# One batch more turned by DMA, named places and a new order in a fused attention and channel-mix kernel

## The chip, the cores and the metric

The kernel runs on one core of a Trainium2 chip. The metric is the device time of one launch in microseconds. The core has a matrix engine (TensorE, PE in the profile, whose weight loads stand apart as PEld), a vector engine (VectorE, DVE), an engine for functions of one element (ScalarE, ACT), GpSimd (POOL) and SyncE (SP). Each has its own instruction stream and works it off in order; they wait for each other through semaphores. Sixteen DMA engines move data. Here POOL issues all loads from HBM, and SP the stores and the transposing transfers.

## The reference

Eight batches, 8 heads, 576 tokens, 64 numbers in each head. First a linear attention with a normalization, then a channel mix over the 512 columns of all heads:

```
kv  = einsum('bhsd,bhse->bhde', k, v)
out = einsum('bhsd,bhde->bhse', q, kv)
x   = out / sqrt(mean(out * out, axis=-1) + 1e-06) * g_norm     # heads side by side: 8 x 576 x 512
x_prev = x shifted by one token, zeros first
xk = mu_k * x + (1 - mu_k) * x_prev
xr = mu_r * x + (1 - mu_r) * x_prev
k2 = max(xk @ w_k, 0)                                           # 512 x 1024
v2 = k2 * k2 @ w_v                                              # 1024 x 512
result = 1 / (1 + exp(-(xr @ w_r))) * v2                        # w_r: 512 x 512
```

Inputs and output are fp32 in HBM; the kernel computes its products in bf16.

## The kernel before

Batches are counted from one in this text and from 0 in the code, so "batch four" is `a == 3`. A batch's 576 tokens are held as 9 groups of 64. Two batches share the buffers of the channel mix: a pair of batches has 9 output tiles of 128 rows, and `V.1.4` in the order means output tile 4 of the pair that batch `1` belongs to.

The work of a batch goes through these steps. The words are those of the order, the functions those of the code.

- `ld.n.b`: one load by POOL, k, v or q (n = 0, 1, 2) of batch b, cast to bf16 on the way (L194). Odd-numbered batches in the code (`b % 2`) lie in three tiles of their own, `in_k`, `in_v` and `in_q`, one each; the even ones reuse `sq0` for k, `qT0` for v and `q0` for q. A load waits until the batch two before it has done with the place.
- `kv`: 72 products of 64x64 on TensorE that make k'v (L287), and `kvo`, two evacuations from PSUM to SBUF.
- q turned, so that its columns lie on the partitions. Batches two to four: `qt`, 72 transposes on TensorE into PSUM (L330), and `qto`, four evacuations. From batch five on (`a >= QD`, with `QD = 4`): `qd`, one transposing DMA from SBUF to SBUF issued by SP (L302), in which pairs of heads come to lie otherwise, so that `kvs` adds a copy of k'v with its upper and lower 64 partitions exchanged (two copies of 64x256, L297). Batch one has code of its own.
- `u`: the products of q and k'v. Without the transposing DMA these are 40 products (L352), with it 72 smaller ones (L316, `u_turned`).
- `sq`, `red`, `nw`, `mul`: squares on ScalarE, their sums, a root by Newton steps and the multiply on VectorE.
- `x`, `xo`, `x0`, `x0o`: the result turned back on TensorE and moved to `xT`; for the last three batches `yd` does this by a transposing DMA (L409) and `gx` multiplies by g.
- `wrap`, `dif`, `sc`, `add`: the token shift and the two mixes xk and xr.
- `K` (`Ka`, `Kz`, `Kp` for the first two batches): products with w_k (L631, L708), each with a relu evacuation on ScalarE or VectorE; `ks` (`ksp`) squares them.
- `R`: product with w_r (L653) and its sigmoid on ScalarE into a tile `sig`.
- `V` (`Vq`): half or quarter of an output tile's product with w_v (L663); `fin` multiplies it by `sig` on VectorE (L676) and has SP store its two halves (L684).
- `L`: the very last output tile, in two column parts of 256 (L671), stored by SP and ACT.
- `wm`: TensorE products that compute nothing, at the start.

The order of all this is written out by hand in `ORDER`, a list of stages made of such words; each word issues its instructions in turn, so this list is the order on every engine and queue. A quote mark behind a word gives the operation to VectorE instead of ScalarE. The digits behind `=` name the PSUM banks that it takes, out of eight. A wait stands where data or a place demand it.

Tiles of the pool `work` rotate: a name has a number of buffers (two as a rule, 7 for `rt`, 6 for `sig`, 7 for `out`), and a new tile takes the one used longest ago.

The places that matter for the change are at the end of the second stage of `ORDER`. The old order has `kv.3`, then `qt.3.1 ... qt.3.0` and their evacuations, `x.2.0.4`, half tiles of `V.1`, and `u.3.1` and `u.3.0` at the beginning of the third stage.

Of the kernel before, what the change touches and what calls it, by code (L numbers as in the profile page):

```python
# [9 lines left out]
FP32 = mybir.dt.float32  # L10
# [9 lines left out]
    cast.0' cast.1' kvc.0.2=01 kvco.1' kvco.0 qtc.0.2=23 qtco.1' cols=4 qtco.0 wm.1.0=1 uc.1=5 sqc.1 uc.0=6  # L20
    qtc.2.2=70 qtco.3' msc.1=1 sqc.0 msc.0=3 qtco.2' rsc.1 wm.1.1=0 kvc.2.1=4 kvco.2 wm.1.2=1 uc.4=2 rsc.0 mcc.1
    uc.2=0 wm.1.3=5 kvc.3.1=7 mcc.0 sqc.2 kvco.3' sqc.4 difh.0.0.256.576 sc.0.0.1.256.576' msc.2=1 uc.3=4
    sc.0.0.0.256.576' uc.5=5 sqc.3 msc.4=3 wm.1.4=7 msc.3=6 rsc.2 add.0.0.0.256.576 wm.1.5=7 Ka.0.4=7 Ka.0.5=1
    rsc.3 mcc.2 mcc.3 dih.0.2.256.576 dih.0.3.256.576 sqc.5 rsc.4 Ka.0.3=6 msc.5=0 fu.0.0.2.256.576 Ka.0.2=4
    fu.0.0.3.256.576 Ka.0.0=3 rsc.5 Ka.0.1=0 Kz.0.4 mcc.4 mcc.5 Kz.0.1 wrap.0 Ka.0.6=2 difh.0.1.0.256 Kz.0.2
    difh.0.0.0.256 sc.0.1.2 Kz.0.0 Kz.0.5' fu.0.0.3.0.256 Ka.0.7=7 fu.0.0.1.0.256 fu.0.0.2.0.256 Kz.0.6 sc.0.1.1
    qt.1.0=50 Kz.0.3' fu.0.0.0.0.256 qto.1.0.1 Kz.0.7 ksp.0.0.0.4' qto.1.0.0' kvh.0=41 kvho.0.0 Kp.0.1.1'=3
    kvho.0.1 Kp.0.1.0'=2 uh.1.0=60 ksp.0.0.4.8 sqh.1.0.0 uh.0.0=74 ld.1.2 uh.2.0=1 sqh.0.1.0 ksp.0.1.0.4'
    sqh.0.0.0 sqh.1.1.0 ld.0.2 sqh.2.0.0 redh.5.9.0 Kp.0.1.2=5 redh.0.5.0 rsh.5.9.0 mulh.0.0.0 Kp.0.1.3=3
    rsh.0.5.0 Vq.0.1.0=2 mulh.0.1.0 ld.2.2 Vq.0.1.1 ksp.0.1.4.8 sc.0.1.3' mulh.2.0.0 Vq.0.2.0=5 qt.1.1=37  # L30
    xh.2.2.0=41 mulh.1.1.0 Vq.0.2.1 xho.2.2.0.0 qto.1.1.1' mulh.1.0.0 qto.1.1.0' xho.2.2.0.1 kvh.1=07 kvho.1.1'
    x0h.0=46 kvho.1.0 x0ho.0.1 x0ho.0.0' xh.0.2.0=13 uh.0.1=07 xho.0.2.0.1' uh.1.1=46 xho.0.2.0.0' sqh.0.0.1
    sqh.0.1.1 uh.2.1=3
    """,
    """
    Vq.0.1.2 add.0.1.1 sqh.2.0.1 sqh.1.0.1 sqh.1.1.1 redh.5.9.1 rsh.5.9.1 Vq.0.2.2 redh.0.5.1 mulh.0.1.1
    Vq.0.3.0=1 rsh.0.5.1 Vq.0.3.1 ld.2.3 mulh.0.0.1 mulh.2.0.1 sc.0.1.0 Vq.0.2.3 Vq.0.3.2 xh.2.2.1=70 add.0.1.0
    mulh.1.0.1 Vq.0.0.0=3 xho.2.2.1.1 mulh.1.1.1 Vq.0.0.1 xho.2.2.1.0 dif.1.384.576 sc.1.0.2.384.576'
    sc.1.0.1.384.576' Vq.0.0.2 sc.1.0.3.384.576 Vq.0.0.3 sc.1.0.0.384.576' adda.1.0.384.576 xh.0.2.1=07
    xho.0.2.1.1' x0h.1=46 x0ho.1.1' xho.0.2.1.0 wrap.1 x0ho.1.0 dif.1.0.384 sc.1.0.3.0.384' Vq.0.3.3  # L40
    sc.1.0.0.0.384' ld.1.3 Vq.0.1.3 tab sc.1.1.3' R.0.1=0 fin.0.1 Kp.1.0.3=4 Kp.1.0.2=7 sc.1.0.2.0.384'
    add.1.0.1.0.384 Kp.1.0.0'=6 sc.1.1.1 Kp.1.0.1'=0 R.0.0=4 sc.1.0.1.0.384' add.1.0.0.0.384 ld.0.3 R.0.2=7
# [12 lines left out]
    K.2.2.1=2 u.3.1=10 fin.1.5 u.3.0=47 u.3.2=3 sq.3.1.1 sq.3.0.0 fin.1.7 add.2.1.0 sq.3.2.0 fin.1.4 sq.3.1.0
    K.2.0.1'=5 K.2.1.1=2 K.2.3.1=6 sq.3.0.1 add.2.1.1 red.3.0.5 red.3.5.9 nw.3.0.1 nw.3.1.2 nw.3.2.3 K.2.6.0=5
    nw.3.3.4 R.2.1=2 ld.2.6 R.2.3=6 nw.3.4.5 K.2.1.0=5 K.2.3.0=2 V.1.8.0=6 nw.3.5.6 nw.3.6.7 K.2.6.1=5 V.1.8.1
    ks.2.1 nw.3.7.8 mul.3.1.0 K.2.5.0=2 mul.3.1.1 mul.3.0.1 mul.3.0.0 mul.3.2.0 K.2.2.0=5 K.2.0.0=1 kv.4=02
    ks.2.0' kvo.4.0 fin.1.8 x.3.0.4=75 x0.3=41 K.2.7.0=3 K.2.5.1=0 kvo.4.1 ks.2.2 ks.2.3' x0o.3.1' xo.3.0.4.1'
    kvs.4.1' R.2.2=6 wrap.3 K.2.4.1=1 xo.3.0.4.0' x0o.3.0' dif.3 sc.3.0.3' sc.3.0.2' sc.3.1.2' K.2.4.0=3 ld.0.6  # L60
    ks.2.4 ks.2.5' R.2.0=5 sc.3.0.1 ks.2.6 sc.3.0.0' V.2.2.0=0 ld.1.6 K.2.7.1=2 add.3.0.1 sc.3.1.0' kvs.4.0
    V.2.0.0=7 V.2.1.0=6 u.4.0=41 u.4.1=35 ks.2.7 qd.5 add.3.0.0 V.2.1.1 sc.3.1.3
    """,
    """
    K.3.4.0'=2 sq.4.1.1 ld.2.7 V.2.0.1 sq.4.0.0 sq.4.0.1 fin.2.0 V.2.2.1 K.3.2.1=2 fin.2.1 fin.2.2 red.4.5.9
    K.3.7.0'=7 sq.4.1.0 K.3.6.0=6 sc.3.1.1 add.3.1.1 K.3.7.1=2 ks.3.7' K.3.2.0=0 K.3.5.0=6 K.3.3.0=7 add.3.1.0
    K.3.4.1=2 u.4.2=0 sq.4.2.0 red.4.0.5 nw.4.0.1 nw.4.1.2 kv.5=67 nw.4.2.3 nw.4.3.4 kvo.5.0 ld.0.7 kvo.5.1
    K.3.0.0=2 nw.4.4.5 K.3.5.1=6 ks.3.4 ld.1.7 nw.4.5.6 kvs.5.0' nw.4.6.7 nw.4.7.8 R.3.6=7 K.3.1.0=2 K.3.0.1=6
    K.3.1.1=7 kvs.5.1' ks.3.5 mul.4.1.0 ks.3.2 mul.4.0.0 K.3.6.1=2 K.3.3.1=6 mul.4.2.0 mul.4.1.1 R.3.7=7
    V.2.3.0=3 mul.4.0.1 ks.3.6' ks.3.0 V.2.3.1 ks.3.3' ks.3.1 x0.4=40 fin.2.3 x0o.4.0 x.4.0.4=25 u.5.2=6  # L70
    u.5.1=71 x0o.4.1' xo.4.0.4.1' u.5.0=43 xo.4.0.4.0 V.3.6.0=0 sq.5.0.1 sq.5.0.0 sq.5.2.0 wrap.4 sq.5.1.0 dif.4
    sc.4.0.3 V.3.6.1 fin.3.6 red.5.5.9 sq.5.1.1 red.5.0.5 V.3.5.0=5 R.3.5=2 nw.5.0.1 nw.5.1.2 sc.4.0.0 qd.6
    sc.4.0.1' nw.5.2.3 V.3.5.1 nw.5.3.4 sc.4.1.3 sc.4.0.2 R.3.4=0 add.4.0.0 V.3.8.0=2 V.3.8.1 nw.5.4.5 R.3.8=0
    fin.3.5 nw.5.5.6 nw.5.6.7 sc.4.1.0 V.3.4.0=5 add.4.0.1 V.3.4.1 nw.5.7.8
    """,
    """
    K.4.7.0=0 mul.5.1.0 mul.5.1.1 K.4.1.1=7 K.4.5.1=1 K.4.4.0=0 mul.5.0.1 mul.5.0.0 mul.5.2.0 sc.4.1.1 add.4.1.0
    K.4.6.0=3 kv.6=74 sc.4.1.2' K.4.4.1=1 ks.4.4 K.4.0.1'=6 K.4.2.0'=0 add.4.1.1 kvo.6.1 K.4.5.0'=3 K.4.2.1'=1
# [40 lines left out]
def kernel(  # L119
# [16 lines left out]
    C = H * HD  # L136
# [689 lines left out]
```

## Time and profile before

| | us |
|---|---|
| median of 3 runs | 199.12 (198.38 to 199.41) |
| the profiled execution, in all | 198.45 |
| its span, from first to last instruction | 196.7 |

The page gives, for each engine, its busy time and its share of the span. TensorE has 2387 products in 185.8 us, VectorE 356 instructions in 163.0 us. The line of the DMA cuts the span into 40 slices of 4.9 us, with the busy share of the sixteen transfer engines in tenths. The chain of waits is followed from the last instruction back to what released it. In a timeline the first number is the start in us from the beginning of the span and the second the duration; a transfer's entry is its issue, not its landing. Groups of instructions are named by line, output and inputs. Some that the change touches, with mean durations of one instruction in this execution:

| group | mean us |
|---|---|
| evacuation of turned q, 128x576: ScalarE / VectorE | 0.645 / 0.450 |
| swapped copy of k'v, 64x256: ScalarE / VectorE | 0.403 / 0.304 |
| last multiply of the output, 128x512 / 128x256 | 0.684 / 0.424 |
| relu evacuation, 128x320, VectorE | 0.490 |
| transposing DMA of y, from issue to landing, with no loads in flight | 4.9 to 6.6 |

### The profile page before, as it was taken

How to read it: one execution, taken by the hardware profiler on the slowest of the kernel's cores; microseconds unless marked ns; L12 is line 12 of the kernel's file. 1: busy time of each engine (PE TensorE's matmuls, PEld its weight loads, DVE VectorE, ACT ScalarE, POOL GpSimd, SP SyncE). 2: the span in 40 equal slices, each digit the busy share in tenths (PEclk: the TensorE clock that was granted, in tenths of full speed). 3: DMA queues.
4: the chain of work that ended last, by engine and by line, in shares of the span. 5: the costliest groups of instructions: out<-in, count | busy, mean ns of one | idle time of the engine just before them, and what ended most of it. 6: DMA issues, size and time to landing. Idle time of an engine off the chain costs nothing.

```text
span 196.7 us, 5776 instructions
## 1 busy us (share of the span) xinstructions
PE 185.8 (94%) x2387; PEld 111.1 (56%) x2409; DVE 163.0 (83%) x356; ACT 134.1 (68%) x275; POOL 27.6 (14%) x44
## 2 busy tenths in 40 slices
PE   7788899999999999999999999999999999999991
PEld 2435565665564667567554775676445666764450
DVE  2488899996999999978999899899899997876241
ACT  2375898779969867969987658989855557532310
POOL 7953343004021004002100000000000000000000
PEclk9999999999999999999999999999999999999999
DMA  5999999999999998999999378335723842005654
GB/s 212 219 211 206 202 205 208 207 217 243 230 230 208 220 189 223 224 170 268 154 215 202 81 136 171 86 80 29 176 45 58 182 107 57 0 0 130 140 144 124
DMA packets 38030, 31.51 MB, mean 160 GB/s; under 512 B 18924, under 2 KB 32500, under 8 KB 38004
## 3 DMA queue, kind: packets, MB, share of 16 engines
q0 software_dynamic: 14400, 16.19, 49.3%
q1 hardware_dynamic: 23204, 14.43, 33.5%
q10 hardware_dynamic: 400, 0.52, 0.8%
q8 instruction: 19, 0.31, 0.6%
q14 instruction: 7, 0.06, 0.1%
HBM read 33.56 MB, written 9.44 MB: 219 GB/s over the span
## 4 chain that ended last, share of the span: by engine, by line
PE 80%; DVE 9%; DMA 4%; issue 2%; ACT 2%; SPq 0%; DVEq 0%; POOLq 0%
PE ps_v L663 28%; PE ps_km L631 28%; PE ps_r L653 15%; DMA q<-in_q_dram 3%; PE ps_kv L287 2%; PE ps_u L316 1%; DVE y L420 1%; PE ps_x L435 1%; DMA out_dram<-out_sb 1%; DVE xT L512 1%; DVE out_sb L676 1%; PE ps_u L352 1%; DVE ss L361 1%; DVE sqk L639 1%; PE ps_qt L330 1%
## 5 line engine op out<-in xcount | busy, mean ns | idle before, releaser
L663 PE MATMUL ps_v<-wv_sb,sqk 128*128 128x512 bf16 x266 | 64.8, 379 | 1.0 <-issue 0.3
L631 PE MATMUL ps_km<-xk,wk_sb 128*128 128x288 bf16 (+3 forms) x480 | 64.0, 285 | 0.0
L631 PEld LDWEIGHTS <-wk_sb 128*128 128x128 bf16 x480 | 45.7, 98 | 16.2
L663 PEld LDWEIGHTS <-sqk 128*128 128x128 bf16 x280 | 26.7, 98 | 29.5 <-issue 0.6
L623 ACT ACTIVATE rt<-ps_km 128x288 bf16<-128x288 f32 (+3 forms) x81 | 33.5, 427 | 12.6 <-PE ps_km L631 9.0
L653 PE MATMUL ps_r<-wr_sb,xr 128*128 128x512 bf16 x136 | 34.9, 379 | 0.5
L656 ACT ACTIVATE sig<-ps_r 128x512 bf16<-128x512 f32 x36 | 21.2, 596 | 18.9 <-PE ps_r L653 18.6
L676 DVE TENSOR_TENSOR out_sb<-ps_v,sig 128x512 f32<-128x512 f32 (+1 forms) x37 | 24.3, 670 | 9.3 <-PE ps_v L663 7.7
L637 ACT ACTIVATE sqk<-rt 128x576 bf16<-128x576 bf16 (+4 forms) x32 | 23.4, 746 | 4.4 <-DVE rt L625 4.2
L601 ACT ACTIVATE m<-dx,cols 128x576 bf16<-128x576 bf16 (+1 forms) x30 | 21.7, 756 | 4.2 <-DVE dx L595 4.0
L625 DVE TENSOR_SCALAR rt<-ps_km 128x288 bf16<-128x288 f32 (+3 forms) x39 | 17.8, 473 | 6.6 <-PE ps_km L631 5.0
L653 PEld LDWEIGHTS <-xr 128*128 128x128 bf16 x144 | 13.9, 98 | 14.2
L361 DVE TENSOR_REDUCE ss<-sq 128x16 f32<-128x1024 bf16 (+1 forms) x12 | 15.8, 1344 | 0.4 <-ACT sq L357 0.4
L357 ACT ACTIVATE sq<-ps_u 128x512 bf16<-128x512 f32 (+1 forms) x30 | 14.6, 556 | 0.0
L618 DVE TENSOR_TENSOR xr<-m,xT 128x1152 bf16<-128x1152 bf16 x16 | 11.9, 750 | 0.8 <-ACT m L601 0.8
L639 DVE TENSOR_TENSOR sqk<-rt 128x576 bf16<-128x576 bf16 (+3 forms) x25 | 11.7, 482 | 0.7 <-ACT rt L623 0.6
L595 DVE TENSOR_TENSOR dx<-xT 128x2304 bf16<-128x2304 bf16 (+5 forms) x13 | 11.4, 893 | 0.4
L603 DVE TENSOR_SCALAR m<-dx,cols 128x576 bf16<-128x576 bf16 (+3 forms) x36 | 11.4, 346 | 0.2
L618 DVE TENSOR_TENSOR xk<-m,xT 128x1152 bf16<-128x1152 bf16 (+2 forms) x16 | 10.9, 699 | 0.2
L420 DVE TENSOR_TENSOR y<-ps_u,rs 128x512 bf16<-128x512 f32 (+1 forms) x15 | 8.4, 628 | 0.1
L217 ACT CAST kv<-ps_kv 128x128 bf16<-128x128 f32 (+1 forms) x15 | 3.3, 244 | 6.9 <-PE ps_kv L472 5.7
L261 PE MATMUL ps_warm<-zeros 128*128 128x512 bf16 x18 | 6.9, 502 | 1.2 <-DVE eps L224 1.2
(91 smaller groups left out, 162.2 us busy)
## 6 DMA issues: line engine op xcount, KB each, us to landing
out_dram<-out_sb SPq DMA_DIRECT2D x67, 128.0 KB, 3.2
qT<-in_v_dram POOLq DMA_DIRECT2D x3, 576.0 KB, 14.4
sq<-in_k_dram POOLq DMA_DIRECT2D x3, 576.0 KB, 12.9
q<-in_q_dram POOLq DMA_DIRECT2D x3, 576.0 KB, 10.8
in_q<-in_q_dram POOLq DMA_DIRECT2D x3, 576.0 KB, 7.9
in_v<-in_v_dram POOLq DMA_DIRECT2D x3, 576.0 KB, 14.3
in_k<-in_k_dram POOLq DMA_DIRECT2D x3, 576.0 KB, 11.8
wk_sb<-in_moe_w_k_dram POOLq DMA_DIRECT2D x2, 512.0 KB, 9.1
```

The costliest lines, as they stand in the source:

```text
L357: ACT.activation(out=sq[:, rg(t0, n, i) if n else slice(0, 1)], in_=held["u", a, part, i][1], func=AF.Square)
L361: DVE.tensor_reduce(out=ss[:, g0:g1], in_=sq[:, g0:g1], op=ALU.add, axis=AX.X)
L601: eng.activation(out=out_, in_=in_, func=AF.Copy, scale=mu)
L618: DVE.tensor_add(out=dst, in0=m[:, hs, c0:c1], in1=x[:, hs, c0:c1])
L623: eng.activation(out=dst, in_=ps, func=AF.Relu)
L625: eng.tensor_scalar(out=dst, in0=ps, scalar1=0.0, scalar2=None, op0=ALU.max)
L631: nc.tensor.matmul(ps[:, n, :], wk_sb[:, cc, 128 * fc:128 * fc + 128], at[b]["xk"][:, cc, c0:c1], start=(cc == 0), stop=(cc == NHP - 1))
L637: eng.activation(out=sqk[:, fcs, o:o + n], in_=src, func=AF.Square)
L653: nc.tensor.matmul(ps, xr[:, cc, 128 * t:128 * t + 128], wr_sb[:, cc, :], start=(cc == 0), stop=(cc == NHP - 1))
L656: ACT.activation(out=sig[b, t], in_=give("r"), func=AF.Sigmoid)
L663: nc.tensor.matmul(ps, sqk[:, fc, 128 * t:128 * t + 128], wv_sb[:, fc, :], start=(fc == 0), stop=(fc == NFC - 1))
L676: DVE.tensor_mul(out=o, in0=give(key), in1=sig[b, t][:, c])
```

## The change

Three things in the functions, and the whole of `ORDER` is written anew.

1. `QD` goes from 4 to 3: batch four's q is turned by the transposing DMA instead of TensorE, its u uses the 72 small products, and its k'v gets the swapped copy.
2. Work tiles get names with a number in them, one buffer to each name: by the parity of the batch for the tiles of a batch, by a list of free numbers for `rt` (7), `sig` (6) and `out` (7), from which a tile takes the number that was given back first.
3. The last output tile is cut into columns 0 to 383 and 384 to 511 instead of two halves. The order takes the smaller one first (`L.1 ... L.0`).

```diff
     def mine(a, key, shape, dtype, tag=None):
         if key not in at[a]:
-            at[a][key] = work.tile(shape, dtype, tag=tag or key, name=tag or key)
+            name = f"{tag or key}{key[1] if tag else a % 2}_"
+            at[a][key] = work.tile(shape, dtype, tag=name, name=name, bufs=1)
         return at[a][key]
...
-    QD = 4
+    QD = 3
...
+    free = {"rt": list(range(7)), "sig": list(range(6)), "out": list(range(7))}
+    place = {}
+
+    def slot(kind, key, shape, dtype):
+
+        n = place[kind, key] = free[kind].pop(0)
+        return work.tile(shape, dtype, tag=f"{kind}{n}_", name=f"{kind}{n}_", bufs=1)
+
+    def leave(kind, key):
+        free[kind].append(place.pop((kind, key)))
...
-            rts[b, fc] = work.tile([128, S], BF16, tag="rt", name="rt", bufs=7)
+            rts[b, fc] = slot("rt", (b, fc), [128, S], BF16)
...
-        c = slice(C // 2 * part, C // 2 * part + C // 2)
+        c = (slice(0, 3 * C // 4), slice(3 * C // 4, C))[part]
```

From the order, what lies around batch four. Before, the end of the second stage and the beginning of the third:

```
... R.1.5=1 mul.2.0.0 R.1.4=7 mul.2.1.0 mul.2.1.1 V.1.4.0=6 x0.2=10 x0o.2.1 kv.3=37 x0o.2.0 ld.1.4 qt.3.1=40
qto.3.1.0' qt.3.0=21 kvo.3.0 ld.2.5 x.2.0.4=35 ksp.1.1.6.8' xo.2.0.4.1' ld.0.5 xo.2.0.4.0 qto.3.0.0
V.1.6.0=4 qto.3.0.1 V.1.6.1 wrap.2 qto.3.1.1 V.1.7.0=5 dif.2 sc.2.1.2' sc.2.0.1 sc.2.0.0 sc.2.1.0 ld.1.5
fin.1.6 sc.2.1.3 sc.2.0.2' sc.2.0.3' V.1.5.0=3 add.2.0.0 kvo.3.1 V.1.4.1 add.2.0.1 V.1.5.1 qd.4 V.1.7.1
sc.2.1.1
--
K.2.2.1=2 u.3.1=10 fin.1.5 u.3.0=47 u.3.2=3 sq.3.1.1 ...
```

After, from the last tile of the first pair to u of batch four and on:

```
... Kp.1.1.4'=1 fin.0.3 u.2.0=63 sq.2.0.0 sq.2.0.1 Kp.1.1.5=0 qd.3 ld.2.4 red.2.5.9 ...
...
nw.2.6.7 nw.2.7.8 ksp.1.1.4.6 V.1.4.0=5 mul.2.0.1 mul.2.1.1 V.1.6.0=0 kv.3=37 mul.2.2.0 mul.2.1.0 x0.2=14
ksp.1.1.6.8 ld.0.5 mul.2.0.0 x.2.0.4=26 kvo.3.1' x0o.2.1' x0o.2.0 xo.2.0.4.0 kvo.3.0' xo.2.0.4.1' wrap.2
kvs.3.1 dif.2 kvs.3.0 V.1.5.0=7 sc.2.0.0 ld.1.5 sc.2.0.1 V.1.4.1 fin.1.4 sc.2.1.2' sc.2.0.2' u.3.0=41
u.3.1=36 sq.3.1.1 sc.2.0.3' sq.3.0.1 sc.2.1.1 V.1.7.0=2 sq.3.1.0 add.2.0.1 V.1.6.1 add.2.0.0 V.1.7.1 V.1.5.1
qd.4 fin.1.7 sc.2.1.3 fin.1.5
```

On SP's queue the transposing DMA of batch four stands behind the eight stores of the first pair's tiles 0 to 3, and that of batch five two stores behind it. The loads of batches three and four stand in the order k, v, q, then k, q, v; before they stood v, k, q, then q, v, k. At the start, the last fused multiply-adds that make xk of batch one's lower columns (`fu.0.0.n.0.256`) stand ahead of the last three `Kz` and their relu evacuations (one on VectorE); before, the last of the four stood behind seven of the eight `Kz`, two of those seven evacuated by VectorE. The number of warm-up products in `wm` goes from 6 to 9. From batch five on the steps are those of before, in another order.

More of the change, by code (lines that the diff above doesn't have):

```diff
@@ L38 @@
[L38 to L42, printed above, removed]
@@ new lines @@
+    add.6.1.0
+    """,
+    """
+    K.6.1.0'=7 K.6.1.1'=1 add.6.1.1 yd.7 K.6.3.0'=6 K.6.2.1=2 K.6.7.0=7 gx.7.0' fin.5.7 K.6.4.0=1 K.6.6.0=2
+    ks.6.1 gx.7.1' K.6.3.1=6 K.6.4.1'=7 K.6.0.1=1 R.6.3=2 K.6.2.0=6 R.6.2=5 wrap.7 V.5.8.0=1 ks.6.2 dif.7
+    K.6.0.0=7 K.6.6.1'=2 sc.7.0.2 sc.7.0.0' sc.7.0.1' add.7.0.0 sc.7.0.3 sc.7.1.3 V.5.8.1 ks.6.3 K.6.5.0=6
+    fin.5.8 add.7.0.1 K.6.5.1=5 R.6.0=7 R.5.5=2 ks.6.0'
+    """,
+    """
+    K.7.5.1'=1 fin.5.5 K.7.6.0=6 K.7.6.1=5 V.6.3.0=7 K.6.7.1'=2 ks.6.7 K.7.7.0'=1 ks.6.6' R.6.1=6 ks.6.4
@@ L109 @@
+    sta.7.7 L.1=2 L.0=0
     """,
@@ L654, in r @@
                              start=(cc == 0), stop=(cc == NHP - 1))
-        sig[b, t] = work.tile([128, C], BF16, tag="sig", name="sig", bufs=6)
+        sig[b, t] = slot("sig", (b, t), [128, C], BF16)
         ACT.activation(out=sig[b, t], in_=give("r"), func=AF.Sigmoid)
@@ L674, in finish @@
     def finish(b, t, key, c=slice(0, C), queues=(nc.sync, nc.sync)):
-        o = outs[b, t] = work.tile([128, c.stop - c.start], FP32, tag="out", name="out_sb", bufs=7)
+        o = outs[b, t, c.start] = slot("out", (b, t, c.start), [128, c.stop - c.start], FP32)
         DVE.tensor_mul(out=o, in0=give(key), in1=sig[b, t][:, c])
@@ L678, in finish @@
             store(b, t, i, q_, c)
+        if c.stop - c.start == C:
+            leave("sig", (b, t))
     outs = {}
@@ L683, in store @@
         bb, j = b - b % 2 + (2 * t + i) // G, (2 * t + i) % G
-        q_.dma_start(out=out[bb].rearrange("(p j) c -> j p c", j=G)[j, :, c], in_=outs[b, t][half(i), :])
+        q_.dma_start(out=out[bb].rearrange("(p j) c -> j p c", j=G)[j, :, c], in_=outs[b, t, c.start][half(i), :])
+        if i == 1:
+            leave("out", (b, t, c.start))
     PARTS0 = ((4 * P, S), (0, 4 * P))
```

136 lines of the change are left out of this document (65 added, 71 removed).

## The prediction

> **What bounds the kernel now.** I read three views in this order: the busy times with the chain of waits, then the timelines of the two engines that issue transfers, then the pieces of the chain around batch four.
>
> The page first. TensorE is busy 94% of the span, and the chain that ended last is 80% TensorE work:
>
> ```profile
> PE 185.8 (94%) x2387; PEld 111.1 (56%) x2409; DVE 163.0 (83%) x356; ACT 134.1 (68%) x275; POOL 27.6 (14%) x44
> ...
> DMA  5999999999999998999999378335723842005654
> ...
> PE 80%; DVE 9%; DMA 4%; issue 2%; ACT 2%; SPq 0%; DVEq 0%; POOLq 0%
> ```
>
> So TensorE work removed anywhere after the start is worth its own time, and a wait of TensorE costs its own length, because its stream is in order. The digits of the DMA say the second thing: until slice 22 (about 108 us) the transfer engines have no free time.
>
> Next, who issues transfers (start, length of the issue, queue, what):
>
> ```profile
> 28.63 0.74 POOL L194 DMA_DIRECT2D in_q<-in_q_dram  x1 [1.56 <-PE ps_x L435]
> ...
> 46.28 0.74 POOL L194 DMA_DIRECT2D q<-in_q_dram  x1 [14.98 <-PE ps_qt L330]
> ...
> 57.69 0.74 POOL L194 DMA_DIRECT2D in_q<-in_q_dram  x1 [9.18 <-PE ps_qt L330]
> ...
> 59.15 0.77 POOL L194 DMA_DIRECT2D in_v<-in_v_dram  x1
> 75.39 0.74 POOL L194 DMA_DIRECT2D q<-in_q_dram  x1 [15.48 <-DMA qT<-q]
> ...
> 76.86 0.77 POOL L194 DMA_DIRECT2D qT<-in_v_dram  x1
> 92.04 0.74 POOL L194 DMA_DIRECT2D in_q<-in_q_dram  x1 [14.41 <-DMA qT<-in_q]
> ```
> ```profile
> 63.01 7.81 SPq L302 DMA_TRANSPOSE qT<-q  x1
> ...
> 77.10 9.88 SPq L302 DMA_TRANSPOSE qT<-in_q  x1
> ```
>
> This gives the price of what the change adds. The transpose of batch five is issued at 63.01, and the load that waits for it goes at 75.39: 12.4 us. That of batch six: 77.10 to 92.04, 14.9 us. Both had loads beside them, v of batch six (issued 59.15, landing 14.3 later) until 73.4, and v of batch seven (76.86, 13.4 later) until 90.2. Each transpose is over 2.0 and 1.8 us after the last of these loads: here it ends when the loads let it.
>
> Last, the chain around batch four (start, length):
>
> ```profile
> 54.97 0.86 PE ps_v L663 x4
> ...
> 56.00 0.71 PE ps_kv L287 x72
> 56.71 0.65 PE ps_qt L330 x72
> 57.36 0.57 PE ps_x L435 x32
> ...
> 64.38 0.49 PE ps_km L631 x4
> 64.87 0.81 PE ps_u L352 x40
> ...
> 82.36 0.67 PE ps_u L316 x64
> ```
>
> k'v at 56.00, the transposes of q on TensorE, and u (q times k'v) only at 64.87.
>
> **The change part by part.** The sum is made against the profiled execution: 198.45 us, a span of 196.7 and 1.75 around it. The median of the three runs is 199.12, 0.67 above it.
>
> (a) The 72 TensorE transposes of q of batch four go: 0.65 us by the chain. With them go four evacuations (0.645 on ScalarE, 0.45 on VectorE each); two swapping copies of k'v (0.403 and 0.304) come. These lie off the chain, beside TensorE work, so I count nothing; uncovered, they would be a gain of 0.5 to 2.0. The 40 products of u become 72 small ones: 0.81 before, 0.67 for 64 of those 72 in the later batches, so 0.75 for all. Together -0.7.
>
> (b) Start. Batch one's lower k columns start at 22.31 on TensorE behind VectorE's last fused multiply-add, 21.70 to 22.17. Two relu evacuations of 0.49 stood in front of it; the new order puts one behind and gives one to ScalarE. VectorE was also idle for 0.94 before the first of them. I take 0.8 of this 0.98 + 0.94; bounds 0 and 1.9. The three added warm-up products (0.2 to 0.4 each) fill TensorE's wait for w_k, which lands at 15.0 in both: 0, and 1.2 if that cover is gone. So -0.8.
>
> (c) The new wait. When does u of batch four come up in the new order? Up to it the old TensorE list has these in addition: the transposes (0.65), four half tiles of the v product (4 x 0.86), one k product (0.49). 64.87 - 0.65 - 3.44 - 0.49 = 60.3; less (b), 59.5. When is its q there? The new list loads k, q, v for batch four where the old one had q, v, k, all issued by 31 and served in turn, so q takes the place of v: 29.82 + 19.9 = 49.7. SP's queue also has to pass the two stores of the tile before, which I put at 49 to 50 (in the old order such stores went at 48.5 to 50.9). So the transpose goes at about 50.0. While it runs, v of batch four and q, k, v of batch five are under way; v of batch five landed at 47.7 + 15.0 = 62.7 with no transpose beside it.
>
> No row shows a transpose at this place, so bounds: 4.9 to 6.6 us to land, as the y transposes (L409) took with no loads beside them: 55 to 57, and no wait. 12.4 and 14.9 from the two rows: 62.4 and 64.9. By the rule that it ends 2 us after the loads, these slowed by some 0.9 each, as from 2.8 us a load (k to v of batch five) to 3.2 to 4.3 beside a transpose: 62.7 + 2.7 + 2 = 67.4. I take 65, the row with three loads beside it. TensorE then stands 65.0 - 59.5 = 5.5 us; bounds 0 and 8.
>
> Behind that u on TensorE stand the four half tiles, then all of the next stage; ScalarE's squares of u, and behind them scale copies of batch three; VectorE runs dry after its sums. All of them wait, so nothing covers this. SP's queue is held by the issue (7.81 and 9.88 in the rows): the stores of the next tiles come later, which seven places for output tiles bear. On POOL the load of q of batch six waits for the same place (57.69 before, 65 now), with k and v behind it.
>
> (d) Order after u. TensorE work left there is the old order's less what (a) removes, plus what (c) lists as postponed, so nothing new. VectorE has some 3 us less work in all (the four evacuations, and copies that go to ScalarE); what it gives TensorE I bound by 0 and the 1.4 us which the old order lost after this point, where tensor work of 126.1 took 127.55. I take 0, as in the stretches from 65 on TensorE is busy nearly throughout.
>
> (e) Tail. Before, the last product of 256 columns is followed by a multiply of 0.42 and a store. Now 128 columns come first and 384 last: the multiply lies between 0.42 (256) and 0.684 (512), say 0.55, and the store, 96 KB for 64, between 2.2 and 2.6 to land. +0.2; bounds +0.1 and +0.6.
>
> (f) Named places. As many as before, handed out to the one freed longest ago, which is what a rotating pool does when the order of release is kept: 0; bounds -0.5 and +0.5, one evacuation either way.
>
> Sum: -0.7 - 0.8 + 5.5 + 0 + 0.2 + 0 = +4.2. 198.45 + 4.2 = 202.6, and by the median 203.3. I write 203.0.
>
> **The rivals.**
>
> The transpose is in time (faster). Its mechanism: the transfer is served like a load of the same size, 7.9 us from issue to landing as q of batch six (57.69) had; 50 + 7.9 = 57.9, before 59.5. Decides from a landing before 59.5. For it: the y transposes at 4.9 to 6.6. Against it: those ran with no loads beside them, and both q transposes that had loads took 12.4 and more. Time: 199.12 - 1.5 + 0.2 = 197.8. The Trainium skill, Advanced Engine Details and Errata, section "X-Bar Transpose (TRN2)", states this case as a rule: transposing DMAs are as fast as regular ones. By it u of batch four would not wait, and the time would be this rival's; this case's trace does not agree with it, at 12.4 and 14.9 us against 7.9 for the plain load.
>
> The wait is small and gives back what the rest gains: landing at 60 to 62, time 198.2 to 200.1. The row of 12.4 us, with an early issue, is just outside.
>
> The wait moves on (slower still): k and v of batch six now go behind q of batch six at 65, and land some 16 us later (57.69 to 73.4 before), at 81. The new order wants them 20.3 us of TensorE work after u, at 85. It decides if they take over 20 us; 3 us more, 206.
>
> The transpose is in time, and the new order starves TensorE elsewhere: VectorE's lead over TensorE at u is some 3 us smaller than in the old order by counting both lists with the mean durations. Time 200 to 202. For it only this count; against it, VectorE's last inputs for u stand early in its list.
>
> **How the numbers follow.** Less than 0.5% either way (1.0 us: 198.1 to 200.1) is what a measurement of this kernel can't tell from no change. Forecast 0.64, its own range 200.6 to 205.6, from landings of 62.5 to 67.5; in time 0.18; small wait 0.10; moves on 0.04; starved elsewhere 0.04. The range must reach into the first rival: 197.2 to 205.6. Faster 0.19, same 0.09, slower 0.72.
>
> **What would show it.** Right: TensorE idle for some 5 us at about 60 to 65, released by the transposing DMA of batch four, and its u right behind; the next q load on POOL waiting for the same DMA. Wrong: u of batch four at 59 to 60 with no wait, or the transpose landing within 9 us of its issue; or it issued well before 49. (b): lower k columns at about 21.5. (e): the last multiply at 0.55.

## The result, and the profile after

| | before | after |
|---|---|---|
| median, us | 198.75 (198.04 to 199.41) | 207.28 (206.81 to 207.67) |
| the profiled execution | 198.45 | 207.67 |
| its span | 196.7 | 205.9 |

The ratio is 1.0429, 95% interval 1.0382 to 1.0475. The direction is the one forecast; the size is not: 203.0 was written, and the time lies above the range.

The page of the changed kernel, the rows of TensorE, of its granted clock and the chain by engine:

```profile
PE   7899899999960999999999999999999999999991
...
PEclk9999999999998599999999999999999999999999
...
PE 74%; DMA 14%; DVE 8%; POOL 1%; issue 1%; SPq 0%; DVEq 0%; POOLq 0%
```

A slice is 5.1 us. Counted from 0, TensorE is busy 6 tenths of slice 11 and none of slice 12, and the clock is at 8 tenths in slice 12 and at 5 in slice 13, where TensorE is busy again. All other slices but the last are at 7 tenths or more, so the loss is in one place. The chain around it (start, length, what):

```profile
49.88 0.90 PE ps_r L665 x4
50.77 16.00 DMA qT__1170<-in_q
66.78 0.04 issue
66.82 1.07 PE ps_u L318 x33
67.89 5.52 PE ps_v L675 x16
73.41 1.47 PE ps_km L633 x12
```

The transposing DMA of batch four is issued at 50.77 and lands 16.0 us later; u stands right behind it. Then come four half tiles of V, 16 products, in 5.52 us: at 0.86 a half tile they would take 3.44. The windows of the same kernel show why (stretch, its length, busy time and instructions of TensorE, its weight loads, VectorE, ScalarE, POOL, then the granted clock, the DMA's share and GB/s):

```profile
58.18:61.59 3.41, 1.67 (x8) 0.58 (x6) 3.27 (x6) 2.79 (x5) 0.00 (x0) 1.00 1.21 199
61.59:65.00 3.41, 0.00 (x0) 0.00 (x0) 1.83 (x4) 0.44 (x1) 0.00 (x0) 1.00 1.34 134
65.00:68.42 3.42, 1.60 (x66) 1.22 (x67) 0.00 (x0) 0.48 (x1) 1.11 (x2) 0.50 1.21 270
68.42:71.83 3.41, 3.41 (x10) 1.22 (x8) 0.00 (x0) 2.42 (x5) 1.87 (x3) 0.50 1.06 157
71.83:75.24 3.41, 3.41 (x30) 2.02 (x28) 2.48 (x5) 1.14 (x4) 0.00 (x0) 1.00 1.20 205
```

TensorE stops at 59.85. At 65.00, 5.2 us later, its clock falls to half, and it stays there until 71.83, five us beyond the end of the wait.

The difference of the spans, 9.2 us, against the forecast's 4.2:

| from the forecast to the trace | us |
|---|---|
| forecast (landing at 65.0, u right behind it) | +4.2 |
| the landing: 66.78, since the issue came at 50.77 and not 50.0 (q at 50.63 and not 49.7), and the DMA took 16.0 and not 15 | +1.8 |
| half clock: the 16 products 2.08 longer, the 64 of u about 0.4 (1.07 against 0.67) | +2.4 |
| what is left, all of it behind u | +0.8 |

In the table of the experiments below the ratio leaves disturbed runs out and the median does not, so the two differ where such runs fell; of e12_gates only the ratio is used, as its profiled run was disturbed.

### The profile page after: what moved, and what is told of

The parts are those of the page before. It is cut to its first block, busy times and chain, and to the rows that moved or that the text cites. A ratio compares the mean times of both kernels' runs of the same rounds, so it can differ in the third digit from the quotient of the medians.

```text
span 205.9 us, 5733 instructions
## 1 busy us (share of the span) xinstructions
PE 190.9 (93%) x2372; PEld 110.8 (54%) x2372; DVE 159.7 (78%) x350; ACT 134.1 (65%) x279; POOL 27.2 (13%) x44
## 4 chain that ended last, share of the span: by engine, by line
PE 74%; DMA 14%; DVE 8%; POOL 1%; issue 1%; SPq 0%; DVEq 0%; POOLq 0%
PE ps_km L633 27%; PE ps_v L675 27%; PE ps_r L665 13%; DMA qT__1170<-in_q 8%; DMA rt<-in_v_dram 3%; PE ps_u L318 2%; PE ps_kv L289 2%; DMA out_dram<-out__3713 1%; DVE xT L514 1%; DVE xk__371 L609 1%; DMA out_dram<-out__3682 1%; PE ps_x L437 1%; DVE dx__357 L597 1%; POOL q L184 1%; DVE xr L620 1%
## 5 line engine op out<-in xcount | busy, mean ns | idle before, releaser
L675 PE MATMUL ps_v<-wv_sb,sqk 128*128 128x512 bf16 x280 | 68.7, 388 | 0.2 <-issue 0.2
L625 ACT ACTIVATE rt<-ps_km 128x384 bf16<-128x384 f32 (+2 forms) x20 | 9.3, 493 | 2.0 <-PE ps_km L724 1.2
L633 PE MATMUL ps_km<-xk__860,wk_sb 128*128 128x192 bf16 (+1 forms) x64 | 9.0, 287 | 0.0
L633 PE MATMUL ps_km<-xk__2035,wk_sb 128*128 128x288 bf16 x64 | 8.8, 286 | 0.0
L633 PE MATMUL ps_km<-xk__2770,wk_sb 128*128 128x288 bf16 x64 | 8.8, 286 | 0.0
L633 PE MATMUL ps_km<-xk__3400,wk_sb 128*128 128x288 bf16 x64 | 8.8, 286 | 0.0
L633 PE MATMUL ps_km<-xk__2527,wk_sb 128*128 128x288 bf16 x64 | 8.7, 286 | 0.0
L633 PE MATMUL ps_km<-xk__3249,wk_sb 128*128 128x288 bf16 x64 | 8.7, 286 | 0.0
L633 PE MATMUL ps_km<-xk__1517,wk_sb 128*128 128x288 bf16 x64 | 8.4, 286 | 0.0
L318 PE MATMUL ps_u<-kv__1285,qT__1170 64*64 64x64 bf16 x72 | 1.4, 234 | 7.0 <-DMA qT__1170<-in_q 7.0
L429 DVE TENSOR_SCALAR xT<-ps_x,cols 128x256 bf16<-128x256 bf16 (+3 forms) x14 | 5.9, 436 | 0.9 <-PE ps_x L437 0.9
L359 ACT ACTIVATE sq__1506<-ps_u 128x512 bf16<-128x512 f32 (+1 forms) x5 | 2.6, 553 | 5.9 <-PE ps_u L318 5.9
L427 ACT ACTIVATE xT<-ps_x,cols 128x64 bf16<-128x64 bf16 (+3 forms) x10 | 5.1, 519 | 1.1 <-PE ps_x L437 1.0
L195 POOL DMA_DIRECT2D in_q<-in_q_dram x3 | 2.2, 745 | 26.3 <-DMA qT__1170<-in_q 19.4
L724 PE MATMUL ps_km<-xk__371,wk_sb 128*128 128x320 bf16 x32 | 5.0, 300 | 0.5 <-DMA wk_sb<-in_moe_w_k_dram 0.2
```

The costliest lines, as they stand in the source:

```text
L195: nc.gpsimd.dma_start(out=x_in[name, b], in_=by_token(dram[name], b))
L318: nc.tensor.matmul(out_, qT_[half(r), b // 2, half(ct % 2)], kv_[half(r), 0 if r == i else 1, ct, :], start=True, stop=True)
L359: ACT.activation(out=sq[:, rg(t0, n, i) if n else slice(0, 1)], in_=held["u", a, part, i][1], func=AF.Square)
L427: eng.activation(out=dst, in_=src, func=AF.Copy, scale=g_sb)
L429: eng.tensor_scalar(out=dst, in0=src, scalar1=g_sb, scalar2=None, op0=ALU.mult)
L625: eng.activation(out=dst, in_=ps, func=AF.Relu)
```

## The experiments

The theory after the result (A): the wait for the transposing DMA and the clock that it brings down are nearly all of the loss, and the DMA is slow because its packets take turns with those of the loads. The main rivals: the new order costs the time by itself (B), or the named places do. Each ratio is against the kernel before on the same chip; the gains in us named below compare medians of different chips, on which the kernel before read 198.5 to 199.5. What is read from a trace holds for the profiled execution.

| run | median, us | ratio (95%) | TensorE's wait at u of batch four |
|---|---|---|---|
| e1_qd4 | 203.57 | 1.019 (1.0102 to 1.0277) | none of the DMA |
| e2_warm | 210.34 | 1.0541 (1.0463 to 1.0618) | 1.9, rest filled |
| e3_late | 202.61 | 1.0175 (1.0112 to 1.0237) | 1.6 |
| e4_gate | 201.41 | 1.0106 (1.0055 to 1.0158) | 0 |
| e5_early | 207.75 | 1.0484 (1.0449 to 1.0519) | 6.5 |
| e6_pool | 207.54 | 1.0447 (1.0432 to 1.0461) | 6.4 |
| e7_turn | 199.61 | 1.005 (1.0035 to 1.0066) | 1.3 |
| e8_apart | 209.21 | 1.0533 (1.0513 to 1.0552) | 1.2, rest filled |
| e9_gate_old | 203.23 | 1.0209 (1.0179 to 1.0238) | 0 |
| e12_gates | | 1.0103 (1.0061 to 1.0146) | |
| e10_late_old | 200.11 | 1.0064 (1.0041 to 1.0087) | 0 |
| e11_ring | 222.55 | 1.1134 (1.1077 to 1.1191) | hidden by another |
| e13_bank | 199.59 | 1.0027 (1.0011 to 1.0043) | 1.6 |
| e14_fill | 199.27 | 1.0046 (1.0013 to 1.0079) | 0 |

### Is it the wait? e1_qd4, e3_late, e4_gate, e6_pool

**e1_qd4**: the new order, with q of batch four on TensorE again.

```
-    QD = 3
+    QD = 4
...
-    Kp.1.1.5=0 qd.3 ld.2.4
+    Kp.1.1.5=0 ld.2.4
...
+    qt.3.0=41 qto.3.0.0 qto.3.0.1' xo.2.0.4.1' wrap.2 qt.3.1=23 ld.2.5 qto.3.1.0 qto.3.1.1'
```

> The new order with batch four's q turned on TensorE again (72 transposes and four evacuations put back, the swapped copies and the transposing DMA taken out), all else as changed. Theory A (the loss is TensorE's wait for the transposing DMA of batch four, 7.0 us, and the 5 us at half clock behind it, worth 2.5): both go and 0.7 of TensorE work comes back, 207.3 - 9.5 + 0.7 = 198.5, with no wait of u of batch four. Theory B (the new order starves TensorE elsewhere too): above 201.

It came between the two. The wait at u is gone; in its place the inserted transposes waited 0.7 us for a PSUM bank, and in this execution the clock stood at half from 9.32 to 12.73 at the start, which the two kernels don't have there. Both theories hold a part: by the ratios (1.019 against 1.0429) somewhat over half of the loss is the DMA's with its clock (a third to three quarters by the interval), and the new order without it is still 1 to 3% slower than before.

**e3_late** moves u of batch four behind the four half tiles of V and two of K.

```
-    sc.2.0.2' u.3.0=41 u.3.1=36 sq.3.1.1 ...
+    sc.2.0.2' ...
...
-    K.2.7.1=5 K.2.6.1=2 K.2.2.0=7 u.3.2=5
+    K.2.7.1=5 K.2.6.1=2 u.3.0=41 u.3.1=36 sq.3.1.1 sq.3.0.1 sq.3.1.0 K.2.2.0=7 u.3.2=5
```

> The changed kernel with u of batch four put 4.4 us later on TensorE, behind the four half tiles and two k products that stood behind it. Theory A: the transposing DMA lands at 66.8 as before, the wait is 7.0 - 4.4 = 2.6 us, too short for the clock to fall (it fell 5.2 us after TensorE stopped), so 207.3 - 4.4 - 2.5 = 200.4. Rival (what makes the time is not covered by other TensorE work): 206 to 207.

The wait fell to 1.6 us, the clock stayed at 1.0, and 4.7 us came back. 2.2 us of the expected gain did not. The trace has new waits for part of it: 0.7 inside V with no releaser, 0.6 of K for ScalarE's evacuation.

**e4_gate** holds POOL's loads of batch five until the transposing DMA has landed (`gate` copies two of its values on POOL, whose queue is in order).

```
-    Kp.1.1.5=0 qd.3 ld.2.4
+    Kp.1.1.5=0 qd.3 gate.3 ld.2.4
```

> The changed kernel with the loads of batch five held on POOL until the transposing DMA of batch four has landed. Theory A3 (the transposing DMA takes 16 us because the loads share the transfer engines with it): it lands 7 to 8 us after its issue, at 58 to 59, u does not wait, no half clock: 207.3 - 9.5 = 197.8, plus up to 2 if k and v of batch five or six, now some 10 us later, come after TensorE wants them: 197.8 to 200. Rival A4 (a transposing DMA of this size takes about 15 us by itself at this place): u waits as before and the time is 207 or more.

The same DMA, issued at 51.21, now landed at 56.71. Its rows among the DMA issues between 51 and 58 us (size, then us from issue to landing), and that of a load issued when it had ended:

```profile
q<-in_q_dram POOLq DMA_DIRECT2D x1, 576.0 KB, 5.7
qT__1170<-in_q SPq DMA_TRANSPOSE x1, 5.5
```

5.5 us against 16.0, and no wait at u. The transpose of batch five in the same run, issued at 63.09 beside five loads, took 19.7. The queues of the changed kernel from 56 to 58 us (queue, packets, MB, share of the sixteen engines):

```profile
q0 software_dynamic: 287, 0.32, 92.6%
q1 hardware_dynamic: 285, 0.07, 27.3%
```

q0 holds the loads, q1 the transpose. One packet of the one goes for one of the other, but those of the loads have 1152 B and those of the transpose 256 B, and it has 2304 of them. While the loads last it sends some 140 per us: 999 from its first packet at 54.86 to 62 us, beside 991 of the loads. Then the loads thin out, and the other 1305 go in 4.3 us. From 62 to 65 us:

```profile
q1 hardware_dynamic: 623, 0.16, 62.7%
q0 software_dynamic: 201, 0.22, 52.5%
```

So the 16.0 us are 4.1 from the issue to the first packet, 7.1 beside the loads, 4.3 for the rest and 0.5 from the last packet to the landing. In e4_gate the same parts are 1.3, then 3.8 for all 2304 packets, and 0.5; between 55 and 56 us, alone, it sent 1135 in one us.

The Trainium skill, Advanced Engine Details and Errata, section "X-Bar Transpose (TRN2)", has transposing DMAs as fast as regular ones: with one load left beside it, e4_gate agrees (5.5 against 5.7 us); beside several loads the traces do not (16.0 us in the changed kernel).

Of the time, 201.4 is less of a gain than expected: the held loads came late for k'v of batch six (0.9 us), and V had stops with no releaser of 1.5 us in all.

**e6_pool** undoes the named places alone.

```
-            name = f"{tag or key}{key[1] if tag else a % 2}_"
-            at[a][key] = work.tile(shape, dtype, tag=name, name=name, bufs=1)
+            at[a][key] = work.tile(shape, dtype, tag=tag or key, name=tag or key)
...
-        return work.tile(shape, dtype, tag=f"{kind}{n}_", name=f"{kind}{n}_", bufs=1)
+        return work.tile(shape, dtype, tag=kind, name=kind, bufs={"rt": 7, "sig": 6, "out": 7}[kind])
```

> The changed kernel with the named places alone undone: kv, qT, x and the like, rt, sig and out come from pools that rotate under one tag, as before the change. Nothing is left out. Theory A (the places cost and bring nothing, all 8.5 us are of the order and the transposing DMA): 207.3 within 0.5. Rival B (a named place is handed on later than a rotating one, so that stores or evacuations hold a product up): under 206.5.

207.54: the places cost and bring nothing.

### What is the clock worth? e2_warm, e8_apart

**e2_warm** puts 24 products that compute nothing ahead of the u that waits.

```
-    sc.2.0.2' u.3.0=41
+    sc.2.0.2' wm.24=4 u.3.0=41
```

> The changed kernel with 24 products that compute nothing on TensorE right ahead of u of batch four: 5.2 us of work inside the 7.0 us of wait. Theory A1 (the half clock after the wait comes from TensorE's idleness): the clock stays at 1.00, u still starts at 66.8, the half tiles behind it take 3.5 us instead of 5.5, and the time is 207.3 - 2.5 = 204.8. Rival A2 (the slow stretch has another cause, for instance the transfers at that time): the half tiles stay at 5.5 us and the time at 207.3.

The clock stayed up at 66 to 72 us, and the third part of u (`u.3.2`) began at 72.48 where the changed kernel has 74.81: 2.33 us, the price of half clock, as expected. But the end came later. At 89.2 TensorE stopped for 3.3 us inside u of batch five, with no releaser, and the clock fell once more (same columns as the windows above):

```profile
87.09:90.50 3.41, 2.12 (x145) 1.54 (x143) 3.41 (x8) 2.76 (x6) 0.00 (x0) 1.00 1.20 199
90.50:93.91 3.41, 1.38 (x9) 0.84 (x11) 1.20 (x2) 0.87 (x2) 0.00 (x0) 1.00 1.31 156
93.91:97.33 3.42, 3.42 (x11) 1.24 (x9) 1.32 (x2) 0.90 (x2) 1.12 (x2) 0.50 0.84 216
```

TensorE idles 1.3 us in the first window and 2.0 in the second, and the third runs at half clock, though TensorE is busy through all of it.

**e8_apart** is e2_warm with the two dense words ahead of that stop (the products of `kv.5` and `u.4`) separated.

```
-    fin.2.1 u.4.0=65 u.4.1=24 add.3.0.1 sq.4.0.1 add.3.0.0 sq.4.0.0 u.4.2=0 sq.4.2.0 ld.1.7 V.2.0.0=3
+    fin.2.1 V.2.0.0=3 u.4.0=65 u.4.1=24 add.3.0.1 sq.4.0.1 add.3.0.0 sq.4.0.0 u.4.2=0 sq.4.2.0 ld.1.7
```

> The kernel of e2_warm (24 warming products ahead of u of batch four, so the clock stays up) with one half tile of V (V.2.0.0, 8 products) moved from behind u of batch five to between kv of batch six and that u. Nothing is left out. In e2_warm TensorE stopped 3.3 us inside that u with no engine busy, and the clock then fell for 3.4 us. Theory A (the stop is TensorE's instruction supply: kv of batch six and u of batch five are 288 small products and weight loads back to back; with 8 long products between them it has time to catch up): no stop over 0.5 us there, no half clock at 94 to 97, 205.0. Rival B (the stop has to do with the moment, a transfer of instructions that meets the loads, not with how dense the words are): a stop of 2 us or more stays near 89 to 92, 208 to 210.

By the numbers B: 209.2, a stop of 2.2 us. But the stop began at 90.2 in place of 89.2 and ended at 92.4, as in e2_warm (92.5). In both, a transfer of 16,384 B on the queue that the page names "instruction" starts at 90.0 to 90.1, 2.4 us before the end of the stop. More work ahead of it shortens the stop from its front, and its end stays with that transfer. The other stops of TensorE over 0.5 us without a releaser, in any of the traces, end alike, 2.4 to 2.6 us after such a transfer began: 0.6 us in e1_qd4, and 0.7 in e3_late, 1.0 in e4_gate and 3.6 in e11_ring inside V with its long products. So dense small products are not needed for it, which speaks against A too. Why the transfer comes no earlier there stays open; that the stop is a wait for instructions is likely, and not shown.

### When does the DMA end? e5_early, e11_ring

**e5_early** loads q first of the batch's three and issues the transpose as soon as it has landed.

```
-    xh.2.2.1=24 ld.0.3 tab mulh.2.0.1 ld.2.3
+    xh.2.2.1=24 ld.2.3 tab mulh.2.0.1 ld.0.3
...
-    fin.0.1 kvo.2.1'
+    fin.0.1 qd.3 kvo.2.1'
...
-    Kp.1.1.5=0 qd.3 ld.2.4
+    Kp.1.1.5=0 ld.2.4
```

> The changed kernel with q of batch four loaded first of that batch's three (before k and v) and its transposing DMA issued behind the stores of fin.0.1, where q should land at 46.0 (the first of the three loads lands there in the changed kernel) instead of 50.6. Nothing is left out. Theory A (the transpose's 2304 packets of 256 B take turns one for one with the packets of the loads, some 140 packets per us beside loads, whenever it is issued): landing 46.1 + 16.5 = 62.6, wait at u of batch four 2.8 us instead of 7.0; that is under the 5.2 us after which the clock fell, so the granted clock stays 1.0 and the 2.4 us of half clock go too: 207.3 - 4.2 - 2.4 = 200.7. Rival B (the transpose ends only when the loads of batch five are through, whenever it starts): landing 65 to 67 as now, wait 5.5 to 7, clock falls, 205.5 to 207.5.

It was issued at 46.15, 4.6 us earlier, and its last packet went at 66.37 where the changed kernel's went at 66.31. As B expected, nothing was won. Between 56 and 58 us its queue sent 298 packets against 289 of the loads, so taking turns holds. What the expectation left out is the lead: its first packet went only at 50.29. From there 2304 packets at 143 per us give 16.1 us, which is the trace. An earlier start only means that it shares for longer: 1864 packets of the loads went between its first and its last, 1188 in the changed kernel. In both it ends soon after the last packet of the loads (66.03 and 65.38). The first packet came right behind the last one of the stores ahead of it on SP's queue (50.16), so I took the queue for the cause.

**e11_ring** puts these stores on ScalarE's queue.

```
     def finish(b, t, key, c=slice(0, C), queues=(nc.sync, nc.sync)):
+        if b == 0:
+            queues = (nc.scalar, nc.scalar)
```

> e5_early with the eight stores of the first batch's output issued on ScalarE's queue instead of SyncE's. Nothing is left out. In e5_early the transposing DMA was issued at 46.15, but its packets began only at 50.0, when the last 2048 B packet of the stores ahead of it in the same queue was through, and it landed at 66.4. Theory A (a queue is first in, first out, and packets of different queues take turns): with the stores in another queue its packets begin at 46.2, share with loads and stores until 50 (about 250 of 2304), then go on at 140 per us: landing 64.5, wait at u 4.5 us instead of 6.5, 205.5, or 203 if the clock stays up. Rival B (it ends when the loads of batch five end, whatever its start): landing 66 to 67, 207.5. ScalarE's eight issues may cost ScalarE some 4 us, which lies beside its evacuations.

That theory fell: issue 46.27, first packet 50.62, landing 66.54. The lead of batch four's transpose is 4.0 to 4.4 us in all runs with several loads in flight, also in e7_turn, where the stores were through at 48.93 and the first packet went at 50.12; in e4_gate with one load left it was 1.3. The time of this run is another matter (what ScalarE and TensorE waited for):

```profile
ACT sq__1163 L359 <- DMA qT__1030<-in_q: 19.3, 1, 19.3
```
```profile
PE ps_r L665 <- ACT rt L625: 17.4, 1, 17.4
```

ScalarE's next store, due at 49.9, waited until 66.56 for the semaphore that the transposing DMA sets (at 66.54), and everything behind it on ScalarE too. The traces show why a store waits for other data: the DMAs of SP and ScalarE take turns on a few semaphores, and the second half of each store waits for the one by which it will tell its own landing. Here that is number 117, the transpose's. In e5_early the transpose had number 114 and this store 117, and nothing waited.

### The DMA in the old order: e7_turn, e10_late_old, e9_gate_old, e12_gates, e13_bank, e14_fill

**e7_turn**: the kernel before with this one part of the change.

```
-    QD = 4
+    QD = 3
...
-    kv.2=26 ksp.1.0.0.8 fin.0.0
+    kv.2=26 ksp.1.0.0.8 fin.0.0 qd.3
...
-    ld.1.4 qt.3.1=40 qto.3.1.0' qt.3.0=21 kvo.3.0 ld.2.5 x.2.0.4=35
+    ld.1.4 kvo.3.0 ld.2.5 x.2.0.4=35
...
-    kvo.3.1 V.1.4.1
+    kvo.3.1 kvs.3.1 kvs.3.0 V.1.4.1
```

> The kernel before with one part of the change alone: q of batch four turned by the transposing DMA, with the swapped copy of k'v; the old order, old places and old last tile are kept. In the old order q of batch four is loaded first and lands at 46.0; the transpose stands behind the stores of fin.0.0 and is issued at about 46.1. Nothing is left out. Theory A (the transposing DMA costs time only where u comes before it lands; 140 packets per us beside loads gives 62.6, and u of batch four, now without the 64 transposes ahead of it, is due at 64.0): no wait over 0.5 us at u, 72 TensorE transposes gone for 32 more small products, 0.5 to 0.8 us less: 198.3, ratio 0.996 to 0.998, unless the loads of batch five that it slows are waited for. Rival B (the transpose lands at 66 or later, or the loads that it slows come late): a wait of 2 us or more, 200.5 to 202.

0.5% slower, where a gain was expected. u comes at 64.7 and waits 1.3 us, as the last packet goes at 65.54. Also, the 0.7 us of the removed transposes do not show: the x product that follows them ends at 58.1, no earlier than before (57.9). TensorE's waits from 55 to 80 us:

```profile
PE ps_u L316 <- DMA qT<-in_q: 1.3, 1, 1.3
PE ps_x L435 <- ACT kv L217: 0.4, 1, 0.4
```

**e13_bank** gives this x a bank that nothing holds.

```
-    x.2.0.4=35
+    x.2.0.4=25
```

> e7_turn with x of batch three (x.2.0.4) given PSUM bank 2 in place of bank 3, which k'v of batch four holds until ScalarE has copied it. Nothing is left out. Theory (the removed transposes stood between k'v of batch four and x of batch three and covered the wait for that bank, 0.4 us): x takes 0.6 us again and starts right behind k'v, 0.3 to 0.5 us earlier at V.1.6; but u of batch four waits for the same landing (65.5), so its wait grows from 1.3 to 1.7 us and the time stays 199.6. The half microsecond shows before u and is gone behind it. Rival (x waits for its y, not for the bank): x still takes 1.0 us or more.

The rival is right: x still takes 1.2 us (56.90 to 58.12), and its wait has another name.

```profile
PE ps_u L316 <- DMA qT<-in_q: 1.6, 1, 1.6
PE ps_x L435 <- DVE y L420: 0.4, 1, 0.4
```

VectorE's five multiplies that make y, the input of x, in the kernel before:

```profile
54.42 2.81 DVE L420 TENSOR_TENSOR y<-ps_u,rs 128x512 bf16<-128x512 f32 x5
```

They end at 57.23, and x began at 57.36 and ended at 57.93. In e13_bank they end at 57.44, and x goes on at 57.50. TensorE's transposes stood where it would have waited for VectorE.

**e10_late_old** puts u behind three more half tiles of K.

```
-    K.2.2.1=2 u.3.1=10 fin.1.5 u.3.0=47 u.3.2=3 ... K.2.0.1'=5 K.2.1.1=2 K.2.3.1=6
+    K.2.2.1=2 fin.1.5 ... K.2.0.1'=5 K.2.1.1=2 K.2.3.1=6 u.3.1=10 u.3.0=47 u.3.2=3
```

> e7_turn with u of batch four moved behind three more half tiles of K (1.5 us of products) and nothing else. Nothing is left out. Theory: the wait of 1.3 us at u goes to 0 to 0.3 and nothing else waits for that u: 198.3, ratio 0.997 to 1.000. Rival (the squares, norms and x of batch four that follow u come 1.5 us later and a product waits for them): 199 to 200.5.

No wait at u, and no gain: K waits 0.7 us for its banks instead, behind VectorE's multiplies of the output. That is the rival's kind of wait, in another place.

**e14_fill** puts a tile of V ahead of u, on top of e13_bank.

```
-    K.2.2.1=2 u.3.1=10 fin.1.5 u.3.0=47 u.3.2=3
+    K.2.2.1=7 V.1.8.0=2 V.1.8.1 u.3.1=10 fin.1.5 u.3.0=47 u.3.2=3
...
-    K.2.3.0=2 V.1.8.0=6 nw.3.5.6 nw.3.6.7 K.2.6.1=5 V.1.8.1
+    K.2.3.0=6 nw.3.5.6 nw.3.6.7 K.2.6.1=2
```

> e13_bank with the tile V.1.8 (two halves, 1.6 us of products) moved from behind u of batch four to ahead of it. Nothing is left out. Theory (what is left of the loss is the wait at u alone): wait at u 0 to 0.3 us, the 0.7 us of the removed transposes are had at last, 198.0 to 198.3, ratio 0.995 to 0.998. Rival (u's five banks and its squares come into the half tiles of K, which then wait for their evacuation as in e10_late_old): 199 to 200.

No wait at u either, 199.27, ratio 1.0046. Again the waits (0.4 for x, 0.5 for K) are for VectorE's y.

**e9_gate_old** and **e12_gates** hold the loads in the old order, as e4_gate did in the new one: of batch five, and then of batch six too.

```
-    nw.2.4.5 ld.2.4
+    nw.2.4.5 gate.3 ld.2.4
```
```
+    V.1.5.1 qd.4 gate.4 ld.2.5 ld.0.5 ld.1.5 V.1.7.1
```

> e7_turn (old order, q of batch four turned by the DMA) with the loads of batch five held on POOL until the transposing DMA has landed. Nothing is left out. In e7_turn the transpose took until after 64.7 and u waited 1.3 us, and the kernel was 1.1 us slower than before. Theory (the transpose goes at some 140 packets per us beside loads and at some 740 alone): issued at 46.1, first packets at about 50 behind the stores in its own queue, beside the loads of k and v until 54, alone from there: landing 57 to 58, no wait at u, 198.0, ratio 0.995 to 0.999; the loads of batch five start at 57 and land by 71, three us ahead of k'v of batch five (74). Rival (what the held loads lose comes back as a wait at batch five or six, whose own transpose then meets the loads): 199 to 201, with a new wait of 0.5 us or more at kv or u there.

> e9_gate_old with the loads of batch six held too until the transpose of batch five has landed. Nothing is left out. If in e9_gate_old the transpose of batch five meets the loads and is late for its u (82), this one has it landed by 73 and reads 198.0; the loads of batch six then run from 73 to 86, before their k'v (90). Rival: POOL's loads of batch six are late in their turn and k'v of batch six waits: 199 to 201.

In e9_gate_old u of batch four found its q (the held loads started at 57.27), and yet the kernel is 2.1% slower, where 198.0 us was expected. The held loads then met the transposes of batches five and six:

```profile
PE ps_u L316 <- DMA qT<-in_q: 2.2, 1, 2.2
...
PE ps_u L316 <- DMA qT<-q: 1.1, 1, 1.1
```

The wait has only moved on, and the clock fell once more at 102.33. With the second gate the ratio is 1.0103, where 198.0 us was expected once more; where the loss lies then is not shown. No version below the kernel before was found.

## Why the forecast was right and wrong

- The views that came first in it hold: TensorE's stream is in order, and nothing covered the wait. The place, the releaser and what waits behind (POOL's load of q of batch six went at 67.31, released by this DMA) are as forecast.
- **(c), the wait**: the mechanism was right, the size somewhat small. u came at 59.85 (59.5 forecast), the issue at 50.77 (50.0), the landing at 66.78 (65): a wait of 7.0 us in place of 5.5, inside the bounds of 0 to 8. The landing was chosen by the row of 14.9 us, and that it came so near is in part luck: the row was of another place with other loads. The rule that was set aside at 67.4 was right in kind. V of batch five landed at 65.83 (65.4 by the rule) and the transpose 0.95 us later (2.0 by the rule); in e5_early, e7_turn and e11_ring, too, its last packet goes 0.3 to 0.4 us after the last one of the loads, whatever its issue.
- **The step that failed** is the sum itself, which prices a wait at its length ("a wait of TensorE costs its own length"). A wait of this length also takes the clock down, and that costs 2.4 us after the wait has ended. No term and no rival had it; without it the time would have been 204.9, inside the forecast range. e2_warm measured it as 2.33, and its clock stayed up when the wait was filled.
- **(a)**, 0.7 us for the transposes: not had where it could be read alone. That they stand on the chain was the wrong test. In the chain before, x follows the transposes with no wait, but its other input, y, was ready at 57.23 and x began at 57.36: the transposes covered VectorE's work but for 0.1 us. e7_turn and e13_bank show the cover. The 72 small products of u took 0.85 and 0.78 us (e7_turn, e14_fill), not 0.75.
- **(b)**, 0.8 at the start: the lower k columns came at 20.79 (21.5 forecast, 22.31 before), yet V.1.4.0, the last tile of that stage that both orders share, starts at 54.79 against 54.81. u of batch two waited 0.5 us for VectorE's k'v in between. For the time it does not matter: what comes before the wait only lengthens it, as the end hangs on the landing. In the sum it was right to subtract it from u's due time; the end was then set by the landing alone.
- **(d)**, 0 behind u: +0.8 was left there, and no single wait over 0.2 us in it. In the changed kernel the wait and the half clock (7.0 + 2.4) already make up the 9.2 us. With the wait gone or cut to 1.6 us (e1_qd4, e4_gate, e3_late) the new order is still 1 to 2% slower than before, in waits whose releasers differ from run to run. What in the order makes them is not shown; no run takes the order apart.
- **(e)** and **(f)** hold: the last multiply takes 0.56 (0.55 forecast), and from TensorE's end to the end of the span it is 4.46 us against 4.24; e6_pool gives the named places 0.
- The rival "in time" asked for the speed of a plain load. With the loads held it has just that, and u does not wait; the kernel was not faster then. The rival "moves on" did not come in the changed kernel; with held loads it did: in e4_gate k'v of batch six waits 0.9 us for its v, in e9_gate_old u of the next two batches waits.

## What to carry to other kernels

A wait on the critical engine is priced at its length plus what its clock does afterwards; look at the granted clock beside the longest wait. A transposing DMA beside loads is priced in parts: the lead to its first packet, its packets at the shared rate while the loads last, and the rest at its own rate. In these runs it ended with the loads, and an earlier start bought little. A removed instruction is worth its time only if the next one's other inputs were there earlier by as much: take their ends from the other engines' timelines, as the chain names only the last.

## What the hardware did that was not expected

**The clock is decided in fixed windows.** In every trace whole multiples of 3.41 us lie between the changes of the granted clock (58.03 and 6.83 in the changed kernel, which are 17 and 2 of them). It fell after a window in which TensorE was idle for 3.41 us (changed kernel), 2.0 (e2_warm, e8_apart) or 2.2 (e9_gate_old), and did not after 1.3 (e2_warm), 1.6 (e3_late), 1.7 (changed kernel) or 1.8 (e6_pool). Once down, it stayed down for one more window after one with 1.8 idle (changed kernel) or 1.6 (e6_pool), so it rises later than it would have fallen. One case at the start does not fit: e1_qd4's fell after a window with 1.2 idle, among the small products of batch one, while e8_apart and e14_fill kept their clock after as much there. So a wait of 7 us always holds a whole window, while one of 3.3 us takes the clock down only if some 2 us of it fall into one. The Trainium skill, TensorE: Matmul & The Clock Gate, section "Part 1: The HAM clock gate (the "warmup" mystery)", has the half rate follow an idle window of about 3.4 us on a free-running grid; the grid agrees, but here a window idle for 2.0 of its 3.4 us was enough.

**The lead of a DMA depends on what is in flight**: 4.0 to 4.4 us from issue to the first packet of batch four's transpose beside several loads, 1.3 with one (e4_gate). That of batch six in the changed kernel had 5.2. Why is not shown.

**Stops without a releaser**, of 3.3 us in e2_warm and 3.6 in e11_ring, ended 2.4 us after a transfer on the queue "instruction" had begun, and the clock fell with each of them; in the changed kernel TensorE does not stop for more than 0.2 us there.
